# New engine lists and a listed buffer order for a packed attention-and-gating kernel

## The chip, the core and the metric

One core of one Trainium2 chip. The metric is the device time of one execution in microseconds (us), as the median of several runs. A profile of one further execution gives the rows that are read below. Five engines work at once: TensorE (PE, the matmuls; PEld are its weight loads), VectorE (DVE), ScalarE (ACT), GpSimd (POOL) and SyncE (SP, which issues nearly all DMAs). Each runs its own list of instructions strictly in the order written; between engines there are only semaphores.

## What is computed

```python
def phi(x):                       # q and k: (4, 4, 1088, 32), r = 8
    a = einsum('rd,bhsd->bhsr', S1, x); b = einsum('rd,bhsd->bhsr', S2, x)
    return einsum('bhsi,bhsj->bhsij', a, b).reshape(..., 64)
q_p, k_p = phi(q), phi(k)
kv = einsum('bhsf,bhsd->bhfd', k_p, v);  z = sum(k_p, axis=2)
x  = (q_p @ kv) / (q_p @ z + 1e-6)            # heads joined: (4, 1088, 128)
h  = maximum(x @ w_in, 0)                     # 1024 wide: u, v of 512 each
v_n = (v - mean(v)) / sqrt(var(v) + 1e-6)
v_s = einsum('ts,bsd->btd', w_spatial, v_n) + b_spatial
out = (u * v_s) @ w_out                       # (4, 1088, 128)
```

The spatial product (1088 x 1088 against 1088 x 512, for each of four batches) is most of the arithmetic.

## The kernel before

**Precision and pieces.** Every float32 operand of a large matmul is split into a high and a low part, and a product is three matmuls: high by high, low by high, high by low. ACT makes the high part by a cast, DVE or POOL the low part by a subtraction. The rows t of the spatial product come in three pieces c: 424, 332 and 332 columns wide; the 512 features in four blocks d; the summed index s in nine tiles kt of 128.

**One block.** For batch b, block d and piece c, `hidden` makes u on PE into the one PSUM bank of the kind `pu`, and ACT moves it to SBUF with a ReLU (`u210:1` is that move for b=2, d=1, c=0). `spatial` adds up nine steps in one of the two banks of the kind `sp` (`sp210:1` to `sp210:9`; a step is three matmuls, the last one two). `gate` multiplies the bank with u on DVE (`u210:2`, line 1173), which frees the bank, and splits the product (`gh210`, `gl210`); `out_mm` multiplies it with w_out (`po20:2` and the like). As there are two `sp` banks, the first step of a block waits for the gate of the block before last.

**Other names.** `pv` are the three matmuls of 512 columns for v, `vt32:1` the ReLU that takes them out of PSUM, `st` and `mv` their statistics, `vt32:4` to `:6` the normalisation, `vh`/`vl` its high and low parts. The two 332-wide pieces of batches 2 and 3 are computed with seven instead of eight products of halves (a Strassen scheme, line 1386); `tw` are the sums of weights for it, `t2`, `t3`, `tx`, `tkp`, `wl` their parts, `s` the sums of v, and `p10` one of the products. `kab`, `qab`, `tq`, `nd`, `xt` and `kv0` are the steps of the attention of batch 0, `pab` of batch 1.

**What sets the order.** `SEQ` is a text of 1904 names with an engine behind each (`u310:2@DVE`). `schedule` splits it into one list for each engine, fixed for good. A loop then walks through the five lists, keeps estimated times, and gives tiles their buffers; its result is the order in which the instructions are written. Where it sees PE waiting in the first 50 us, it puts matmuls of nothing (line 607) in between. The buffers of a kind are given out in one order for that kind:

```python
ts[:] = sorted((t for t in ts if t.users), key=lambda t: RANK.get(t.name, (t.users[0].n, t.users[0].first.index(t))))
```

With `RANK` empty this is the order in which the program text first uses the tiles.

Of the kernel before, what the change touches and what calls it, by code (L numbers as in the profile page):

```python
# [66 lines left out]
kv0:3@PE wt00:1@SP qab01:1@PE wt80:1@SP wi_x1:5@DVE tq00:1@PE kd0:1@DVE qa01:1@ACT wi_x1:6@DVE tq01:1@PE qpT00:1@ACT qab02:1@PE qp01:1@DVE qpT01:1@ACT
wi_x1:7@POOL qa02:1@ACT nd00:1@PE wi_x0:1@ACT qp02:1@DVE v93:1@POOL wih:1@ACT wi_x0:2@DVE tq10:1@PE rec0:1@DVE wil:1@POOL tq11:1@PE rec0:2@DVE
x320:1@DVE qpT10:1@ACT tq20:1@PE qpT11:1@ACT wi_x0:3@DVE xt0:1@PE nd01:1@PE xh0:1@ACT wi_x0:4@DVE xl0:1@DVE tq21:1@PE rec1:1@DVE pv000:1@PE rec1:2@DVE
wi_x0:5@DVE x321:1@DVE qpT20:1@ACT wTh:9@ACT qpT21:1@ACT bh:1@ACT wTh:1@ACT wTl:10@SP pv001:1@PE wi_x0:6@DVE wTh:2@ACT wt30:1@SP xt1:1@PE vt00:1@ACT  # L70
bl:1@DVE wt60:1@SP wi_x0:7@DVE nd02:1@PE vt00:2@ACT wt01:1@SP st000:1@DVE wTl:1@POOL xh0:2@ACT wt11:1@SP wTh:3@ACT xl0:2@DVE wt21:1@SP pv002:1@PE
wih:2@ACT rec2:1@DVE wTl:3@POOL eps:2@DVE wt31:1@SP rec2:2@DVE mv00:1@DVE pv010:1@PE x322:1@DVE wt70:1@SP vt00:3@ACT st001:1@DVE wt41:1@SP xt2:1@PE
wil:2@POOL vt01:1@ACT pv011:1@PE st002:1@DVE xh0:3@ACT mv00:2@DVE pv012:1@PE xl0:3@DVE wTl:9@POOL vt01:2@ACT mv00:3@DVE st010:1@DVE pu000:1@PE
sd00:1@ACT wTh:10@ACT qt10:1@SP st011:1@DVE wTl:2@POOL pv020:1@PE vt01:3@ACT qt11:1@SP u000:1@ACT rs00:1@DVE qt12:1@SP st012:1@DVE pv021:1@PE
# [4 lines left out]
vl00:3@DVE sp030:2@PE vt01:6@DVE sd02:1@ACT sp010:2@PE vh00:4@ACT vt01:5@DVE sp010:3@PE abT11:1@ACT sp000:3@PE rs02:1@DVE vl00:4@DVE vh00:5@ACT
sp020:1@PE wo_x:1@ACT t102:1@DVE sp030:3@PE wTl:12@DVE sp030:4@PE wTh:5@ACT t102:2@DVE vl00:5@DVE wt71:1@SP sp000:4@PE wTh:8@ACT qd10:2@SP sp020:2@PE  # L80
rs02:2@DVE vh00:6@ACT nm02:1@DVE sp020:3@PE vt02:4@DVE sp020:4@PE wTh:6@ACT vt02:5@DVE sp010:4@PE vh00:7@ACT vl00:6@DVE sp020:5@PE wTh:15@ACT
sp010:5@PE wTl:8@DVE wTh:13@ACT sp010:6@PE wo_x:2@DVE vt02:6@ACT sp030:5@PE vl00:7@DVE sp020:6@PE vh00:8@ACT sp030:6@PE wTl:6@DVE wTh:7@ACT sp000:5@PE
v90:2@POOL wTl:17@DVE sp000:6@PE wTh:12@ACT sp030:7@PE vh00:9@ACT vl00:8@DVE sp000:7@PE wt81:1@SP wTh:17@ACT sp020:7@PE vh00:10@DVE qd10:1@SP
wTh:16@ACT sp010:7@PE v92:2@ACT wTl:14@DVE sp030:8@PE wTl:15@DVE sp000:8@PE wt02:1@SP sp000:9@PE wTl:7@DVE sp020:8@PE wt12:1@SP wTl:19@DVE sp010:8@PE
sp000:10@PE wTl:5@DVE wt22:1@SP sp020:9@PE wTh:18@ACT sp000:11@PE wTl:18@DVE sp030:9@PE wTh:14@ACT sp020:10@PE sp010:9@PE wo_x:3@DVE v93:2@ACT
wt32:1@SP sp010:10@PE wTh:11@ACT wTl:16@DVE sp000:12@PE sp010:11@PE qd11:2@SP sp000:13@PE wTl:13@DVE wTh:19@ACT sp010:12@PE sp000:14@PE wo_x:4@DVE
qd11:1@SP abT12:1@ACT sp030:10@PE v91:2@ACT sp000:15@PE sp030:11@PE sp010:13@PE wt42:1@SP wo_x:5@DVE sp000:16@PE sp030:12@PE wt52:1@SP wo_x:6@DVE
sp010:14@PE sp020:11@PE sp030:13@PE wTl:20@DVE sp030:14@PE sp020:12@PE sp030:15@PE wo_x:7@POOL wt62:1@SP sp000:17@PE sp020:13@PE sp020:14@PE kt10:1@SP
sp010:15@PE sp000:18@PE kt11:1@SP sp030:16@PE sp010:16@PE u000:2@DVE wTl:21@POOL sp010:17@PE kt12:1@SP sp020:15@PE sp020:16@PE g000:1@ACT sp010:18@PE
sp020:17@PE woh:1@ACT sp030:17@PE u010:2@DVE sp001:1@PE wol:1@DVE sp001:2@PE g010:1@ACT sp001:3@PE wTh:20@ACT g000:2@DVE v10:1@SP sp001:4@PE  # L90
g010:2@DVE wt72:1@SP sp001:5@PE wTh:25@ACT wTl:22@DVE sp030:18@PE u030:1@ACT sp020:18@PE wTl:27@DVE sp001:6@PE wt82:1@SP wTh:22@ACT u020:2@DVE
po00:1@PE fa100:1@SP u030:2@DVE po00:2@PE v11:1@SP g020:1@ACT wTl:24@DVE pu001:1@PE g030:1@ACT g020:2@DVE fb100:1@SP kab10:1@PE g030:2@DVE fb100:2@SP
v12:1@SP po00:3@PE ka10:1@ACT u001:1@ACT po00:4@PE wTh:21@ACT wTh:23@ACT pu011:1@PE ob00:1@ACT kp10:1@DVE wTl:25@DVE sp011:1@PE ka11:1@ACT out:1@SP
wTh:26@ACT sp011:2@PE ka12:1@ACT fa101:1@SP wTl:28@DVE wTh:24@ACT sp001:7@PE u011:1@ACT kp11:1@DVE fa100:2@POOL sp001:8@PE fb101:2@SP wTh:27@ACT
sp011:3@PE fb101:1@SP wTl:29@DVE sp011:4@PE fh100:1@ACT sp011:5@PE fa110:1@SP fl100:1@POOL sp011:6@PE fb110:1@SP kp12:1@DVE sp011:7@PE fb110:2@SP
sp011:8@PE sp011:9@PE qd12:1@SP sp001:9@PE u011:2@DVE kv1:1@PE fa111:1@SP u001:2@DVE fa101:2@POOL fb111:1@SP pu021:1@PE kd1:3@DVE kd1:4@DVE kd1:1@DVE
sp021:1@PE qd12:2@SP kd1:2@DVE u021:1@ACT sp021:2@PE kvh1:1@ACT fb111:2@SP gh001:1@ACT sp031:1@PE kvl1:1@DVE fh101:1@ACT sp031:2@PE gl001:1@DVE
gh011:1@ACT sp031:3@PE fl101:1@POOL sp031:4@PE sp031:5@PE wTl:26@POOL nd100:1@PE fa120:1@SP nd101:1@PE fa110:2@POOL x3210:1@ACT fb120:2@SP po01:1@PE
x3210:2@ACT pu031:1@PE xn10:1@ACT fa121:1@SP x3210:3@DVE sp031:6@PE fh110:1@ACT kt20:1@SP sp031:7@PE xn10:2@ACT fl110:1@POOL fb120:1@SP sp021:3@PE
sp031:8@PE fa111:2@POOL fb121:2@SP sp021:4@PE sp021:5@PE kt21:1@SP x3210:4@DVE sp021:6@PE fb121:1@SP gl011:1@DVE sp021:7@PE xh1:1@ACT sp021:8@PE  # L100
fh111:1@ACT xl1:1@DVE sp031:9@PE u031:1@ACT fl111:1@POOL sp021:9@PE po01:2@PE u021:2@DVE pv100:1@PE fa120:2@POOL gh021:1@ACT pv101:1@PE gl021:1@DVE
vt10:1@ACT pu002:1@PE st100:1@DVE vt10:2@ACT pv102:1@PE st101:1@DVE nd110:1@PE vt10:3@ACT u031:2@DVE po01:3@PE mv10:1@DVE fh120:1@ACT nd111:1@PE
fl120:1@POOL sp002:1@PE x3211:2@ACT sp012:1@PE u002:1@ACT wTl:23@POOL sp012:2@PE x3211:1@ACT sp002:2@PE x3211:3@DVE fa121:2@POOL sp002:3@PE sp002:4@PE
fh121:1@ACT sp012:3@PE xn11:2@ACT fl121:1@POOL sp002:5@PE gh031:1@ACT sp002:6@PE xn11:1@ACT sp012:4@PE x3211:4@DVE sp002:7@PE xh1:2@ACT sp002:8@PE
xl1:2@DVE sp012:5@PE gl031:1@DVE sp012:6@PE sp002:9@PE sp012:7@PE u002:2@DVE pu012:1@PE st102:1@DVE pv110:1@PE mv10:2@DVE mv10:3@DVE pv111:1@PE
vt11:1@ACT gh002:1@ACT po01:4@PE st110:1@DVE vt11:2@ACT pv112:1@PE sd10:1@ACT st111:1@DVE ob01:1@ACT sp022:1@PE u012:1@ACT rs10:1@DVE sp022:2@PE
# [1500 lines left out]
```

## Time and profile before

| what | value |
|---|---|
| device time, median of 3 runs (lowest to highest) | 318.24 us (317.87 to 319.25) |
| the profiled execution | 320.65 us |
| its span, first to last instruction | 318.8 us |
| busy share of PE, DVE, ACT, POOL | 97%, 73%, 57%, 31% |
| mean granted clock of TensorE | 0.994 of full speed |

The profiled execution has 1.85 us outside its span, and took 2.4 us more than the median. A matmul's end is modelled in the profile, so that neighbours overlap; how far PE gets is read from the distance between two starts.

### The profile page before, as it was taken

The page shows a single profiled execution, that of the slowest core. Times are in us where ns is not written, and L with a number is a line of the kernel's source. Part 1 is how long each engine was busy: PE and PEld are TensorE (multiplying, and loading weights), DVE is VectorE, ACT ScalarE, POOL GpSimd, SP SyncE. Part 2 cuts the span into 40 slices and gives each one's busy share as a digit, 9 for nine tenths or more (in the row PEclk, how much of TensorE's full clock was granted, in tenths as well). Part 3 has the DMA queues.
Part 4 walks back from the last instruction along what each step waited for, and adds up shares of the span by engine and source line. Part 5 has one row for each costly group of instructions (what it writes and reads, how often), then busy time and mean ns, then how long its engine had stood idle before and what let it go on. Part 6 is the DMA issues. An engine that isn't in the chain of part 4 may idle for free.

```text
span 318.8 us, 6893 instructions
## 1 busy us (share of the span) xinstructions
PE 309.7 (97%) x2602; PEld 296.7 (93%) x2602; DVE 231.4 (73%) x525; ACT 182.7 (57%) x428; POOL 98.2 (31%) x130
## 2 busy tenths in 40 slices
...
GB/s 245 237 80 319 61 127 220 191 115 103 60 65 45 40 119 159 102 7 92 48 142 236 179 180 256 37 83 43 59 1 2 27 298 1 94 90 2 2 0 70
DMA packets 22989, 33.78 MB, mean 106 GB/s; under 512 B 3116, under 2 KB 21420, under 8 KB 22956
## 3 DMA queue, kind: packets, MB, share of 16 engines
...
q8 instruction: 20, 0.33, 0.4%
...
## 4 chain that ended last, share of the span: by engine, by line
PE 88%; DVE 5%; ACT 2%; DMA 2%; issue 1%; SPq 0%; ACTq 0%; DVEq 0%
PE sp L1136 14%; PE sp L1145 12%; PE sp L1138 12%; PE sd L1386 8%; PE sp L1386 7%; PE sd L575 3%; PE sd L577 3%; PE sd L576 3%; PE pu L575 2%; PE sp L1147 2%; PE po L575 2%; PE po L576 2%; PE po L577 2%; PE pu L577 2%; PE pu L576 2%; PE sd L787 2%
## 5 line engine op out<-in xcount | busy, mean ns | idle before, releaser
L1136 PE MATMUL sp<-wTh,vh 128*128 128x332 f32 (+1 forms) x286 | 94.2, 331 | 1.8 <-DVE u L1173 1.8
L1138 PE MATMUL sp<-wTh,vl 128*128 128x332 f32 (+1 forms) x240 | 79.1, 330 | 0.0
L1136 PEld LDWEIGHTS sp<-wTh,vh 128*128 128x128 f32 x286 | 54.3, 190 | 2.6 <-DVE u L1173 2.1
L1138 PEld LDWEIGHTS sp<-wTh,vl 128*128 128x128 f32 x240 | 45.4, 189 | 0.2
L1145 PE MATMUL sp<-wl,vh 128*128 128x332 f32 x128 | 39.6, 309 | 0.0
L1145 PE MATMUL sp<-wTl,vh 128*128 128x424 f32 x112 | 39.2, 354 | 0.0
L1173 DVE TENSOR_TENSOR u<-sp,u 128x332 f32<-128x332 f32 (+1 forms) x43 | 22.4, 523 | 18.8 <-PE sp L1147 12.8
L1129 ACT ACTIVATE u<-pu 128x332 f32<-128x332 f32 (+1 forms) x44 | 20.6, 469 | 17.4 <-PE pu L577 14.3
L978 DVE BATCH_NORM_STATS2 st<-vt 128x6 f32<-128x512 f32 x36 | 24.1, 685 | 9.0 <-ACT vt L976 8.9
L976 ACT ACTIVATE vt<-sd 128x512 f32<-128x512 f32 x36 | 21.3, 599 | 13.0 <-PE sd L577 12.6
L583 DVE TENSOR_TENSOR g<-u,g 128x332 fp32r<-128x332 f32 (+1 forms) x41 | 24.6, 599 | 5.1 <-ACT g L662 2.4
L953 DVE RECIPROCAL c<-c 128x384 f32<-128x384 f32 (+1 forms) x9 | 21.7, 2415 | 7.1 <-ACT c L951 7.0
L586 POOL TENSOR_TENSOR r<-pl,r 128x384 fp32r<-128x384 f32 (+1 forms) x18 | 17.5, 973 | 28.5 <-DVE g L583 11.3
L662 ACT CAST g<-u 128x332 fp32r<-128x332 f32 (+1 forms) x41 | 20.0, 488 | 10.6 <-DVE u L1173 8.0
L919 POOL TENSOR_TENSOR pl<-pl,pl 128x384 f32<-128x384 f32 (+1 forms) x18 | 17.4, 972 | 25.2 <-DMA pl<-qd 13.4
L1145 PEld LDWEIGHTS sp<-wl,vh 128*128 128x128 f32 x128 | 24.0, 188 | 0.0
L1050 ACT CAST vh<-vt 128x384 fp32r<-128x384 f32 x44 | 21.9, 511 | 1.6 <-DMA vt<-vd 1.5
L1052 POOL TENSOR_TENSOR vl<-vt,vh 128x384 fp32r<-128x384 f32 (+1 forms) x15 | 14.6, 979 | 23.7 <-ACT vh L1050 22.7
L1145 PEld LDWEIGHTS sp<-wTl,vh 128*128 128x128 f32 x112 | 21.3, 190 | 0.1
L1052 DVE TENSOR_TENSOR vl<-vt,vh 128x384 fp32r<-128x384 f32 (+1 forms) x29 | 17.2, 603 | 1.1 <-ACT vh L1050 1.1
L575 PE MATMUL pu<-xh,wih 128*128 128x332 f32 (+1 forms) x48 | 16.3, 339 | 1.1 <-ACT u L1129 0.9
L1394 DVE TENSOR_TENSOR sp<-sp,pl 128x332 f32<-128x332 f32 x24 | 12.2, 510 | 6.5 <-PE sp L1147 6.3
...
## 6 DMA issues: line engine op xcount, KB each, us to landing
...
```

The lines of the kernel that those rows point to most:

```text
L575: nc.tensor.matmul(o, ah, bh, start=start, stop=False)
L576: nc.tensor.matmul(o, ah, bl, start=False, stop=False)
L577: nc.tensor.matmul(o, al, bh, start=False, stop=stop)
L583: return lambda: nc.vector.tensor_tensor(out=o(), in0=a(), in1=bb(), op=ALU.subtract)
L978: op("DVE", 690, lambda stats=stats, t=t: nc.vector.bn_stats(out=stats.ap, in_=vt[:, t]), r=[(vt, t)], w=[stats])
L1050: op("ACT", c_act(384), lambda: nc.scalar.copy(out=vh[:, kk:kk + 3], in_=x()), r=vr, w=[(vh, g)])
L1052: return lambda: eng.tensor_tensor(out=vl[:, kk:kk + n], in0=x()[:, :n], in1=vh[:, kk:kk + n].bitcast(F32), op=ALU.subtract)
L1136: nc.tensor.matmul(sp[:, :cw], vh[:, kt], wTh[:, kt, cs], start=(kt == begin), stop=False)
L1138: nc.tensor.matmul(sp[:, :cw], vl[:, kt], wTh[:, kt, cs], start=False, stop=False)
L1145: nc.tensor.matmul(sp[:, :cw], vh[:, kt], w_lo(kt, c), start=False, stop=False)
L1173: op("DVE", c_dve(cw), lambda: nc.vector.tensor_tensor(out=u.ap, in0=sp[:, :cw], in1=u.ap, op=ALU.mult), r=[sp], w=[u])
L1386: nc.tensor.matmul(x[:, :cw], p, q, start=i == 0 and n == 0, stop=end and i == 3 and n == 2)
```

## The change

The same 1904 operations are issued. What differs is their order in all five lists, which engine does 118 of them (47 go from POOL to DVE, 43 from DVE to POOL, 12 from ACT to DVE, 8 from DVE to ACT, 4 from POOL to ACT, 4 from ACT to POOL), and `RANK`, which now lists the order in which the tiles of five kinds of buffers (kp, c, vl, g and r) are given out. The number of buffers, the tile shapes and the functions stay. The places that are spoken of below, from the new and the old text of `SEQ`, and a part of `RANK`:

```diff
--- before.py
+++ after.py
@@ -60,152 +60,172 @@
 AFTER_W = (7.0, 13.0, 13.0)
 
 SEQ = """
...
-kab02:1@PE ka02:1@ACT wi_raw0:1@SP wi_x1:4@DVE qab00:1@PE b32:1@SP kv0:1@PE kp02:1@DVE qa00:1@ACT wt20:1@SP eps:1@ACT kv0:2@PE wt10:1@SP qp00:1@DVE
...
-mv02:1@DVE nm00:1@DVE mv01:1@DVE wt61:1@SP mv01:2@DVE wTh:4@ACT vt00:4@DVE pu020:1@PE wt40:1@SP vt02:3@ACT st021:1@DVE wTl:4@POOL pab10:1@PE wt50:1@SP
-u020:1@ACT st022:1@DVE vh00:1@ACT pu030:1@PE vt00:5@DVE sd01:1@ACT abT10:1@ACT pab11:1@PE rs01:1@DVE vl00:1@DVE vh00:2@ACT pab12:1@PE vt00:6@ACT
...
-pu200:1@PE st310:1@DVE vt31:2@ACT pv312:1@PE tw5756:1@SP u200:1@ACT mv31:1@DVE vt30:5@DVE out:5@SP nd320:1@PE u200:2@DVE vt31:3@ACT xd1:1@SP
-pu210:1@PE vt30:4@DVE vt30:6@ACT nd321:1@PE tw1424:2@DVE x3232:1@ACT sp220:1@PE st311:1@DVE vh30:1@ACT sp220:2@PE st312:1@DVE x3232:2@ACT
-tw1756:2@POOL u210:1@ACT sp220:3@PE vh31:1@ACT tw5756:2@DVE sp210:3@PE wTh:29@ACT vh21:4@DVE sp220:4@PE mv31:3@DVE t2h0:1@ACT tw5424:2@POOL mv31:2@DVE
-x3232:3@DVE sd31:1@ACT sp210:4@PE xn32:1@ACT v91:4@POOL t3h0:1@ACT sp220:5@PE tw4424:2@POOL gh200:1@ACT sp210:5@PE xn32:2@ACT vh22:4@POOL sp220:6@PE
-rs31:1@DVE t131:1@DVE t131:2@DVE x3232:4@DVE sp210:6@PE rs31:2@DVE xh3:3@ACT sp220:7@PE nm31:1@DVE t3h1:1@ACT xl3:3@DVE sp220:8@PE vt31:6@ACT
-xh3:4@POOL sp210:7@PE xl3:4@POOL vt31:4@ACT sp210:8@PE t2h1:1@ACT sp210:9@PE vt31:5@ACT sp220:9@PE pv320:1@PE pu220:1@PE vt32:1@ACT pv321:1@PE
-txh:1@POOL pv322:1@PE vl30:1@POOL vl31:1@DVE wl1:1@DVE t2l0:1@DVE tw2424:1@SP txh:2@DVE out:6@SP tw2756:1@SP u210:2@DVE tw6424:1@SP gl200:1@DVE
-u220:1@ACT st320:1@DVE vt32:2@ACT tw6756:1@SP vh30:2@ACT pu300:1@PE st321:1@DVE vt32:3@ACT po20:1@PE tw2424:2@POOL u220:2@DVE gh210:1@ACT sp300:1@PE
-s100:1@DVE vh32:1@ACT sp300:2@PE u300:1@ACT mv32:1@DVE mv32:2@DVE vl30:2@DVE vh31:2@ACT sp310:1@PE st322:1@DVE tw2756:2@POOL sp310:2@PE mv32:3@DVE
-sp300:3@PE t2l1:1@POOL sd32:1@ACT wih:3@ACT rs32:1@DVE gl210:1@DVE sp310:3@PE gh220:1@ACT tw3424:1@SP pu310:1@PE t132:1@DVE tw6756:2@DVE p10:1@PE
-t132:2@DVE rs32:2@DVE p10:2@PE nm32:1@DVE vt32:4@ACT vt32:6@DVE p10:3@PE vt32:5@DVE p10:4@PE t2h2:1@ACT vl31:2@DVE sp300:4@PE vh31:3@ACT v90:5@POOL
-u310:1@ACT po20:2@PE vl31:3@DVE vh33:1@ACT wil:3@POOL sp310:4@PE vh31:4@DVE t3h2:1@ACT sp310:5@PE vh30:3@ACT txh:3@POOL txl:1@ACT sp300:5@PE
-vh32:3@ACT sp310:6@PE s300:1@POOL v91:5@ACT tw3756:1@SP vh33:3@ACT sp310:7@PE s100:2@POOL sp300:6@PE v92:5@POOL vh31:5@ACT sp310:8@PE tw6424:2@POOL
-wTh:30@ACT vh32:2@ACT vl32:2@POOL vl33:1@DVE gl220:1@DVE vl32:1@DVE vl30:3@DVE vl32:3@DVE tkp1:1@DVE vh30:4@DVE tw7424:1@SP po20:3@PE sp310:9@PE
-sp300:7@PE u310:2@DVE sp300:8@PE wl2:1@POOL vh32:4@DVE sp320:1@PE tw7756:1@SP sp320:2@PE t2l2:1@DVE tw3424:2@DVE sp300:9@PE wo_raw3:1@SP vl31:4@DVE
...
+ka01:1@ACT kp01:1@DVE kab02:1@PE kv0:1@PE ka02:1@ACT wi_raw0:1@SP qab00:1@PE kp02:1@DVE wt00:1@SP qa00:1@ACT wt80:1@SP eps:1@ACT qp00:1@DVE kv0:2@PE
...
+wTh:2@ACT mv01:1@DVE nm00:1@DVE pu010:1@PE vt00:4@DVE wt70:1@SP vt02:1@ACT vt00:6@DVE pv021:1@PE vh00:1@ACT vt00:5@DVE u010:1@ACT pv022:1@PE
+vl00:1@DVE vt02:2@ACT pu020:1@PE st011:1@DVE wTl:2@POOL vt02:3@ACT sp000:1@PE st012:1@DVE vh00:2@ACT sp010:1@PE wTl:12@POOL u020:1@ACT st020:1@DVE
+sp030:1@PE sp020:1@PE mv01:3@DVE mv01:2@DVE vl00:2@POOL pab10:1@PE st021:1@DVE sd01:1@ACT wTh:14@ACT pab11:1@PE rs01:1@DVE st022:1@DVE abT10:1@ACT
...
+sp200:9@PE sp210:5@PE tw5756:2@DVE u210:1@ACT u200:2@DVE nd320:1@PE vt30:6@ACT vt30:4@DVE nd321:1@PE x3232:1@ACT pu220:1@PE mv31:2@DVE wl1:1@DVE
+x3232:2@ACT tw5424:2@DVE sp220:1@PE t2h0:1@ACT tw2424:1@SP x3232:3@DVE gh200:1@ACT sp220:2@PE t2l0:1@POOL vh30:1@ACT sp210:6@PE t2h1:1@ACT tw2756:1@SP
+vh31:1@ACT sp210:7@PE t3h0:1@ACT sp220:3@PE t3h1:1@ACT st312:1@DVE sp210:8@PE xn32:2@ACT txh:2@POOL xn32:1@ACT mv31:3@DVE vl30:1@DVE sp220:4@PE
+sd31:1@ACT u220:1@ACT sp220:5@PE tw6424:1@SP x3232:4@DVE sp220:6@PE xh3:3@ACT sp210:9@PE xl3:3@DVE sp220:7@PE u210:2@DVE xl3:4@POOL sp220:8@PE
+xh3:4@POOL rs31:1@DVE gh210:1@ACT t131:1@DVE sp220:9@PE t131:2@DVE txl:2@ACT rs31:2@DVE sp300:1@PE nm31:1@DVE gl200:1@DVE pv320:1@PE vt31:5@DVE
+vl31:1@DVE pu300:1@PE vt32:1@ACT s300:1@DVE pv321:1@PE vt31:4@DVE u300:1@ACT vt31:6@ACT st320:1@DVE tkp1:2@POOL pv322:1@PE u220:2@DVE vt32:2@ACT
+pu310:1@PE t2l1:1@POOL tw6756:1@SP vh31:2@ACT st321:1@DVE sp300:2@PE vt32:3@ACT tw2424:2@POOL tw3424:1@SP sp310:1@PE st322:1@DVE p10:1@PE wTh:30@ACT
+mv32:2@DVE p10:2@PE s100:1@DVE mv32:1@DVE po20:1@PE mv32:3@DVE vl31:2@DVE sd32:1@ACT wih:3@ACT sp310:2@PE rs32:1@DVE vh32:1@ACT t132:1@DVE gl210:1@DVE
+sp300:3@PE txl:1@ACT tw2756:2@DVE u310:1@ACT sp310:3@PE tw6756:2@DVE vh30:2@ACT sp310:4@PE t132:2@DVE t2h2:1@ACT rs32:2@DVE wil:3@DVE sp310:5@PE
+nm32:1@DVE txh:1@DVE vt32:5@ACT pu320:1@PE vl30:2@DVE tw3756:1@SP gh220:1@ACT vt32:6@DVE p10:3@PE vh33:1@ACT vt32:4@DVE p10:4@PE tkp1:1@DVE sp300:4@PE
+vh32:3@ACT vl32:1@DVE vh31:3@ACT tw7424:1@SP po20:2@PE vl33:1@DVE v91:5@ACT sp310:6@PE vh30:3@ACT vl31:3@DVE v93:4@ACT sp300:5@PE vl30:3@DVE
+t3h2:1@ACT vh31:4@DVE vh33:2@ACT wl2:1@DVE sp300:6@PE vh32:2@ACT vh30:4@DVE tw7756:1@SP sp310:7@PE txh:3@DVE v90:5@ACT gl220:1@DVE sp300:7@PE
+wo_raw3:1@SP tw3424:2@DVE sp310:8@PE vl32:2@DVE sp310:9@PE vl32:3@DVE sp300:8@PE u310:2@DVE vh32:4@POOL sp300:9@PE vl33:2@DVE po20:3@PE t2l2:1@DVE
+sp320:1@PE u300:2@DVE sp320:2@PE tw6424:2@DVE gh300:1@ACT s100:2@DVE sp320:3@PE v92:5@ACT tw3756:2@DVE wTh:31@ACT sp320:4@PE vh31:5@ACT gl300:1@DVE
...
 """.split()
 
-RANK = {}
+RANK = {
+    "kp00": 0, "kp01": 1, "kp02": 2, "qp00": 3, "qp01": 4, "qp02": 5, "u000": 6, "u010": 7, "u020": 8, "u030": 9, "ob00": 11, "kp10": 10, "kp11": 12,
+    "kp12": 13, "kd1": 14, "kp20": 15, "kp21": 16, "kp22": 17, "kd2": 18, "kp30": 19, "kp31": 20, "kp32": 21, "kd3": 22, "tkp1": 23, "tkp0": 24,
...
+    "tkp2": 25, "qt00": 0, "qt01": 1, "qt02": 2, "qpT00": 3, "qpT01": 4, "x320": 6, "qpT10": 5, "qpT11": 7, "x321": 10, "qpT20": 8, "qpT21": 9,
+    "x322": 11, "qt10": 12, "qt11": 13, "qt12": 14, "x3210": 15, "xn10": 16, "x3211": 18, "xn11": 19, "x3212": 21, "xn12": 22, "qt20": 17, "qt21": 20,
...
+    "t2h3": 39, "gh231": 40, "gl231": 41, "gh232": 42, "gl232": 43,
+}
 
 END = B - 2
 LATE_GATES = {(END, 3, 1), (END, 3, 2)}
```

## Rows read from the trace of the kernel before

**Rows 1.** The page's first part: busy us, share and instructions of each engine.
```profile
PE 309.7 (97%) x2602; PEld 296.7 (93%) x2602; DVE 231.4 (73%) x525; ACT 182.7 (57%) x428; POOL 98.2 (31%) x130
```

**Rows 2.** Stretches: length; busy of PE, PEld, DVE, ACT, POOL (instructions); clock, DMA, GB/s.
```profile
9.02:31.62 22.60, 22.29 (x312) 18.05 (x311) 21.19 (x56) 18.89 (x43) 9.49 (x9) 1.00 0.65 207
31.62:206.22 174.60, 174.60 (x1533) 168.94 (x1532) 124.92 (x268) 108.93 (x252) 57.14 (x69) 1.00 0.38 117
196.28:211.04 14.76, 13.83 (x74) 13.02 (x73) 11.41 (x26) 11.56 (x25) 7.22 (x10) 1.00 0.38 123
211.04:225.32 14.28, 13.14 (x73) 12.79 (x71) 13.31 (x28) 8.77 (x22) 8.49 (x10) 1.00 0.09 25
218.15:224.61 6.46, 6.03 (x33) 5.69 (x31) 6.38 (x7) 3.60 (x10) 6.44 (x7) 1.00 0.09 26
226.43:229.84 3.41, 3.41 (x12) 3.19 (x11) 1.68 (x4) 1.62 (x4) 0.90 (x1) 0.50 0.33 94
```

**Rows 3.** Timeline of PE: start us, length us, instruction, idle time before and what ended it.
```profile
9.52 0.71 PE L607 MATMUL po<-u 128*128 128x128 f32 x4
...
29.41 0.55 PE L896 MATMUL sd<-c,sk 128*64 128x192 f32 x4
...
31.62 0.46 PE L1136 MATMUL po<-wTh,vh 128*128 128x424 f32 x1
...
193.07 0.31 PE L575 MATMUL po<-g,woh 128*128 128x332 f32 x1
...
208.63 0.40 PE L577 MATMUL sd<-wih,xl 128*128 128x512 f32 x1
209.96 0.46 PE L575 MATMUL pu<-xh,wih 128*128 128x424 f32 x1 [0.93 <-ACT u L1129]
...
211.21 0.35 PE L1136 MATMUL sp<-wTh,vh 128*128 128x424 f32 x1
...
214.57 0.35 PE L575 MATMUL pu<-xh,wih 128*128 128x424 f32 x1
...
223.84 0.35 PE L1145 MATMUL sp<-wTl,vh 128*128 128x424 f32 x1
225.97 0.46 PE L1136 MATMUL sp<-wTh,vh 128*128 128x424 f32 x1 [1.79 <-DVE u L1173]
```

**Rows 4.** The chain that ended last, in order of time: start us, us, what.
```profile
26.24 0.23 PE sd L577
...
241.22 1.78 PE sd L1386 x12
```

**Rows 5.** Timeline of DVE around the two waits of PE.
```profile
196.28 0.59 DVE L1173 TENSOR_TENSOR u<-sp,u 128x424 f32<-128x424 f32 x1
196.79 0.54 DVE L1014 TENSOR_SCALAR vt<-vt,mv,sm 128x512 f32<-128x512 f32 x1
197.25 0.50 DVE L1216 TENSOR_TENSOR pl<-pl,pl 128x332 f32<-128x332 f32 x1
197.66 1.28 DVE L978 BATCH_NORM_STATS2 st<-vt 128x6 f32<-128x512 f32 x2
...
200.38 2.12 DVE L953 RECIPROCAL c<-c 128x320 f32<-128x320 f32 x1
...
204.33 0.55 DVE L1052 TENSOR_TENSOR vl<-vt,vh 128x384 fp32r<-128x384 f32 x1
204.80 0.54 DVE L1216 TENSOR_TENSOR wl<-pl,wTh 128x332 fp32r<-128x332 f32 x1
...
207.75 0.51 DVE L1216 TENSOR_TENSOR xh<-pl,kt 128x332 fp32r<-128x332 f32 x1 [1.96 <-ACT vt L976]
...
220.49 3.26 DVE L1052 TENSOR_TENSOR vl<-vt,vh 128x384 fp32r<-128x384 f32 x3
...
225.32 0.60 DVE L1173 TENSOR_TENSOR u<-sp,u 128x424 f32<-128x424 f32 x1
```

251 lines of the change are left out of this document (126 added, 125 removed), and 14 rows, old and new, of the table RANK.

## The prediction

> **What bounds the kernel now.** The page's first part comes first: PE is busy 97% of the span, DVE 73%, ACT 57%, POOL 31% [rows 1]. All lists hold the same matmuls before and after, so time can come only from where PE stands still, runs at the lower clock or does filler. The stretches tell where that is [rows 2]. From 31.62 to 206.22 PE is busy for all of 174.60 us: nothing can be gained there, only lost. In the timeline of PE [rows 3] two waits follow. At 208.63 a matmul of 512 columns starts and the next one 1.33 us later; at 223.84 one of 424 columns starts and the next 2.13 us later. A matmul's own step is the distance of two starts: from 211.21 to 214.57 there are 18 of 424 columns, 0.187 us each [rows 3]; one of 512 columns takes 0.23, one of 332 takes 1.78 / 12 = 0.148 [rows 4]. So the waits cost 1.1 and 1.94 us. After the second the granted clock is 0.50, the 1.2 GHz level, from 226.43 to 229.84 [rows 2]. Half of these 3.41 us, 1.7, is what the clock costs. After the first wait the stretch from 211.04 to 225.32 shows 1.00.
>
> Why PE waits is seen in the timeline of DVE [rows 5]. The second wait ends 0.65 us after the gate at 225.32 starts, which is `u310:2`; `sp320:1` needs its bank. Since the gate at 211.04 (`u220:2`, where a stretch of rows 2 begins) 14.28 us had passed. In the middle, from 218.15 to 224.61, POOL is busy for 6.44 of 6.46 us with seven instructions [rows 2], and DVE's three `vl` at 220.49 take 3.26 us, where one alone takes 0.47 (204.33 to 204.80) [rows 5]: DVE is stretched by POOL. The first wait ends with ACT's `u220:1`, which needed a buffer that `gl200:1` frees; on DVE that stood behind `txh:2` at 207.75, which had idled for 1.96 us [rows 5].
>
> **The change, part by part.** `RANK` adds no instruction; it allows other orders, and where the buffers come free is in the lists. The five lists decide.
>
> *First wait.* In the new list `pu220:1` stands ahead of `sp220:1`, so that nine steps of `sp220` (8 x 0.56 + 0.37 = 4.9 us) and more lie between it and `pu300:1`; `txh:2` has gone to POOL. The price of `u220:1` is hidden under them. I take the 1.1 us as gone. Bounds: 1.1 back, if `gl200:1` is late, or nothing.
>
> *Second wait.* I set DVE's work from `u200:2` to `u310:2` against PE's from the end of `sp200:9` to `sp320:1`. Steps on DVE, by distance of starts [rows 5]: a 424-wide operation 0.51 (196.28 to 196.79), a normalisation 0.46, a 332-wide subtraction 0.41, statistics 0.64 (1.28 / 2), a 384-wide `vl` 0.47, the reciprocal 2.1. Estimates from these: 0.35 for 256 wide, 0.3 for `vh..:4`, 0.1 for the tiny ones. From `u200:2` up to `u220:2` the new list has 23 operations: three 424-wide 1.53, three normalisations 1.38, seven tiny 0.7, four of 332 or 320 wide 1.64, the reciprocal 2.1, two statistics 1.28, two `vl` 0.94, one 256-wide 0.35: 9.9 us. From there up to `u310:2` there are 34: three 424-wide 1.53, two statistics 1.28, eight tiny 0.8, five `vl` 2.35, seven 332-wide 2.87, five 256-wide 1.75, two normalisations 0.92, two `vh..:4` 0.6: 12.1. With the gate and its way to PE, 0.65, that is 22.7 us.
>
> PE has, up to the end of `sp220:9`, 43 matmuls of 424 columns and 6 of the small `nd32` (0.147): 8.9 us; from there 70 of 424 (13.1), nine of 512 (2.1) and twelve of 332 (1.8): 17.0. Together 25.9, which leaves DVE 3.2 us for three things. Its late start: PE moved on from `sp200:9` at 193.07 [rows 3], and the gate began at 196.28 [rows 5], 3.2 us late; the least is about 0.2 (a hand-over between the engines, an estimate). Between the gates of `sp132` and `sp200` the new list has 21 operations, at DVE's mean of 231.4 / 525 = 0.44 us [rows 1] 9.2 us, against some 12 us of matmuls; I take 0.6. Its waits: the old list idled 14.76 - 11.41 = 3.35 us and 14.28 - 13.31 = 0.97 [rows 2]; without the 1.96 of `txh:2` that is 2.4, which I take; least nothing. POOL beside it: the old list has ten POOL instructions in the second of these stretches, the new one two (`t2l1:1`, `tw2424:2`), and five in the first. DVE's seven operations from 218.15 to 224.61 were worth some 2.7 us by the steps above and were busy 6.38 [rows 2]: 3.7 us lost to 6.44 us of POOL, 0.57 for each. At a mean of 0.72 us (7.22 / 10, rows 2) the two cost 0.8; all seven, with 5.0 us, 2.9; none, nothing. I take 1.1, as in the first stretch POOL's 7.22 us [rows 2] left the steps of rows 5 at their usual size. The sum is 0.6 + 2.4 + 1.1 = 4.1 against 3.2: PE waits 0.9 instead of 1.94. Gain 1.0; bounds 1.94 (no wait) and a loss (below).
>
> *The clock.* A wait of about 0.9 us is like the first one, after which the clock stayed at 2.4 GHz. So the 1.7 us go too. If the wait is like the second one, they stay.
>
> *The head.* Before 31.62 PE works with short gaps. `kv0:1` now stands before `qab00:1`, where four filler matmuls took 0.5 us [rows 3]; the first spatial steps stand ahead of `pab10:1`, and from 29.41 to 31.62 [rows 3] PE did some 1.6 us of work (`pab` 1.05, `pu030` 0.56) in 2.2: 0.6 to be had. Against it, `wil:1` comes to DVE, and DVE is busy 21.19 of 22.60 us there [rows 2]; a 512-wide subtraction is some 0.6 (an estimate from 0.47 at 384), and it lies ahead of the first `xl0`. Bounds: 1.1 gained, 0.6 lost; I take a gain of 0.2, a little under the middle.
>
> *Elsewhere* 80 other operations change engine under 174.60 us of unbroken PE. I take nothing; the cover is that DVE is busy 124.92 and ACT 108.93 of these [rows 2]. If the cover is gone in one place, it costs a wait like the first, 1.1. At the end the last steps keep their order: nothing.
>
> **A rule that speaks against it.** The rows show that POOL stretches DVE by about 0.57 us for each us, when the two lie beside each other [rows 2, 5]. The Trainium skill, page "SBUF — State Buffer", section "Who interferes with whom", says that a DVE instruction with two SBUF inputs and a GpSimd instruction that reads SBUF block each other wholly, whichever starts second. By that rule POOL's whole 5.0 us of the new stretch could fall on DVE: PE would wait 0.6 + 2.4 + 5.0 - 3.2 = 4.8 us instead of 1.94, the lower clock would stay, and with the first wait gone and 0.2 from the head the time would be 318.24 + 2.9 - 1.1 - 0.2 = 319.8. The trace agrees only in part: from 196.28 to 211.04 POOL is busy for 7.22 us [rows 2], and the steps beside it keep their size [rows 5].
>
> **Sum.** 1.1 + 1.0 + 1.7 + 0.2 = 4.0. The profiled execution would go from 320.65 to 316.7. The median of the runs is 2.4 below it, so part of these losses may be absent there; I take off the whole: 318.24 - 4.0 = **314.2 us**. Without the part of the clock it would be 315.9.
>
> **The rivals.**
> - *DVE is as late as before.* The new list moves work from POOL onto DVE, from 8.6 us (26 operations at the same steps) to 12.1 between the last two gates; what POOL no longer takes away, DVE now does itself. Then the wait at `sp320:1` and the lower clock stay, and only the first wait goes: 318.24 - 1.1 = 317.1, or 316.9 with the head. For it: the margin of 3.2 us is no more than the old waits alone, 2.4, with little else. Against it: the old list gave away 0.97 idle and 3.7 to POOL in that stretch.
> - *DVE is later than before (slower).* The place is the same, `sp320:1`. If all 5.0 us of POOL fall on DVE, with the old late start of 3.2 and the waits of 2.4, the sum is 10.6 against 3.2: PE waits 7.4. With 1.94 and 1.1 gone and the clock's 1.7 staying, 318.24 + 4.4 = 322.6. It decides from where late start, waits and POOL reach 3.2 + 1.94 + 1.1 + 1.6 = 7.8 us. Against it, POOL's 7.22 us from 196.28 to 211.04 cost DVE next to nothing [rows 2, 5]. The rule of the page "SBUF — State Buffer" of the Trainium skill would make it likelier.
> - *Everything goes.* No wait at `sp320:1`, and the head gives 1.0: 318.24 - 1.1 - 1.94 - 1.7 - 1.0 = 312.5.
> - *The lists don't do what they say*, since the estimates by which they were chosen miss the chip's times. The new list would then wait in places that were unbroken, 1.1 or 2.1 us each: three of the former undo the gain, 317.5.
>
> **Chances.** Forecast 0.45; everything goes 0.2; as late as before, or undone by new waits, 0.23; slower 0.12. A change of under 0.5% (1.6 us: 316.65 to 319.83) is about what this kernel's measurement can't tell from none. The first two are faster by more: 0.65; the third is the same for nearly all: 0.23; slower 0.12. The range leaves out 1 in 10 at each end: from 312.3 (a little under "everything goes") to 319.6. The forecast's own range is 313.0 to 316.0.
>
> **What would show it.** Right: no wait ahead of `pu300:1`; the wait ahead of `sp320:1` under 1 us; a granted clock of 1.00 from 190 to 240; DVE's operations near 0.5 us each between `u220:2` and `u310:2`; the first spatial step earlier than 31.62. Wrong: a PE wait of 1.8 us or more around the gates of 200 to 230 us, a stretch at 0.50, or waits between 32 and 206, where there were none.

## The result, and the profile after

The kernel after takes 315.16 us (median of six executions, 313.96 to 316.06), the kernel before in the same comparison 319.01 (six, 317.87 to 320.37): a ratio of 0.9875, interval 0.9842 to 0.9909. 314.2 had been forecast. The profiled execution of the kernel after took 313.96 and was the fastest of its six, that of before took 320.65, more than any of its six; so the traces differ by 6.7 us where the medians differ by 3.85.

Page of the kernel after, first part, and from the second part the busy tenths of PE and the granted clock in 40 slices:

```profile
PE 306.6 (98%) x2598; PEld 295.3 (95%) x2598; DVE 228.7 (73%) x533; ACT 179.0 (57%) x424; POOL 93.0 (30%) x126
...
PE   7999999999999999999999999999999999999995
...
PEclk9999999999999999999999999999999999999999
```

Against [rows 1] DVE is busy for 2.7 us less and POOL for 5.2. No slice of PE but the first and the last is below nine tenths, and no clock is low. What PE still waits for is in the view of its waits (us in total, times, longest); all three lie in the first 14 us:

```profile
PE sd L618 <- DVE u L612: 1.3, 1, 1.3
PE sd L770 <- DMA kt<-in_kT: 0.4, 1, 0.4
PE pu L807 <- issue: 0.3, 1, 0.3
```

Stretches of the kernel after, columns as in [rows 2]: all that follows the head up to the end of `sp220`, from `u200:2` to `u220:2`, and from there to `u310:2`:

```profile
32.06:205.69 173.63, 173.63 (x1526) 168.07 (x1525) 122.80 (x260) 105.17 (x245) 58.65 (x73) 1.00 0.40 122
197.67:208.94 11.27, 11.27 (x61) 10.82 (x60) 10.57 (x25) 8.82 (x21) 2.58 (x5) 1.00 0.16 45
208.94:221.78 12.84, 12.84 (x73) 12.81 (x72) 12.41 (x35) 9.38 (x24) 2.26 (x3) 1.00 0.26 76
```

The second and third answer to the two stretches of [rows 2] that took 14.76 and 14.28 us. DVE now idles 0.70 and 0.43 us in them (before: 3.35 and 0.97), and POOL is busy for 4.84 us in both together (before: 15.71).

Timeline of PE after, at the two places of [rows 3]: `pu300:1` at 206.94 and `sp320:1` at 222.67 start 0.23 and 0.18 us after the matmul ahead of them, their plain steps.

```profile
206.71 0.39 PE L597 MATMUL sd<-wih,xl 128*128 128x512 f32 x1
206.94 0.35 PE L595 MATMUL pu<-xh,wih 128*128 128x424 f32 x1
...
222.49 0.35 PE L597 MATMUL po<-g,wol 128*128 128x424 f32 x1
222.67 0.35 PE L1156 MATMUL sp<-wTh,vh 128*128 128x424 f32 x1
```

Timeline of DVE after, against [rows 5]: `gl200:1`, `u220:2`, four `vl` in a row and `u310:2`. The four take 1.77 us now, where three took 3.26.

```profile
206.11 0.59 DVE L603 TENSOR_TENSOR g<-u,g 128x424 fp32r<-128x424 f32 x1
...
208.94 0.58 DVE L1193 TENSOR_TENSOR u<-sp,u 128x424 f32<-128x424 f32 x1
...
216.66 1.77 DVE L1072 TENSOR_TENSOR vl<-vt,vh 128x384 fp32r<-128x384 f32 x4
...
221.78 0.60 DVE L1193 TENSOR_TENSOR u<-sp,u 128x424 f32<-128x424 f32 x1
```

Of the signs that the prediction named, those of the waits, the clock and DVE's lengths came. The first spatial step came earlier too, at 28.41, as `sp000:1` now stands ahead of `pab10:1`; but the 31.62 of before was itself late. With the same old head it starts at 30.78 to 31.12 in the seven other traces that have it, here h3's; and before waited longer for the DMA of `kt` (first view; 0.3 to 0.5 us in three of the seven, none in four):

```profile
PE sd L750 <- DMA kt<-in_kT: 1.1, 1, 1.1
```

```profile
30.86 0.46 PE L1136 MATMUL po<-wTh,vh 128*128 128x424 f32 x1
```

### The profile page after: what moved, and what is told of

Same layout as the page of the kernel before. It is cut to its first block, busy times and chain, and to the rows that moved or that the text cites. A ratio compares the mean times of both kernels' runs of the same rounds, so it can differ in the third digit from the quotient of the medians.

```text
span 312.2 us, 6880 instructions
## 1 busy us (share of the span) xinstructions
PE 306.6 (98%) x2598; PEld 295.3 (95%) x2598; DVE 228.7 (73%) x533; ACT 179.0 (57%) x424; POOL 93.0 (30%) x126
## 4 chain that ended last, share of the span: by engine, by line
PE 94%; DMA 2%; SPq 1%; DVE 0%; ACT 0%; issue 0%
PE sp L1156 15%; PE sp L1158 13%; PE sp L1165 13%; PE sd L1406 9%; PE sp L1406 7%; PE sd L595 4%; PE sd L597 4%; PE sd L596 4%; PE pu L595 3%; PE pu L597 3%; PE po L595 3%; PE pu L596 3%; PE po L596 2%; PE po L597 2%; PE sp L1167 2%; PE sd L807 2%
## 5 line engine op out<-in xcount | busy, mean ns | idle before, releaser
L1158 PE MATMUL sp<-wTh,vl 128*128 128x424 f32 (+1 forms) x240 | 78.8, 328 | 0.0
L1165 PE MATMUL sp<-wTl,vh 128*128 128x424 f32 x112 | 38.1, 349 | 0.0
L603 DVE TENSOR_TENSOR g<-u,g 128x332 fp32r<-128x332 f32 (+1 forms) x41 | 22.3, 543 | 8.3 <-PE po L597 3.8
L1072 POOL TENSOR_TENSOR vl<-vt,vh 128x384 fp32r<-128x384 f32 (+1 forms) x15 | 13.5, 904 | 14.4 <-ACT vh L1070 9.4
L1072 DVE TENSOR_TENSOR vl<-vt,vh 128x384 fp32r<-128x384 f32 (+1 forms) x29 | 16.1, 569 | 1.7 <-ACT vh L1070 1.7
L777 DVE TENSOR_TENSOR kp<-ka,sd 128x768 f32<-128x768 f32 x15 | 13.9, 951 | 4.5 <-ACT ka L775 4.3
```

Of the source, the lines that this page charges most:

```text
L603: return lambda: nc.vector.tensor_tensor(out=o(), in0=a(), in1=bb(), op=ALU.subtract)
L1072: return lambda: eng.tensor_tensor(out=vl[:, kk:kk + n], in0=x()[:, :n], in1=vh[:, kk:kk + n].bitcast(F32), op=ALU.subtract)
L1158: nc.tensor.matmul(sp[:, :cw], vl[:, kt], wTh[:, kt, cs], start=False, stop=False)
L1165: nc.tensor.matmul(sp[:, :cw], vh[:, kt], w_lo(kt, c), start=False, stop=False)
```

## The experiments

Theory: the change gains because DVE is in time for the two waits at 208 and 224 us, and all else in the lists is worth nothing in sum. Rivals: the head gives about 1 us; or DVE's work is what it is, so that a wait taken away in one place comes back in the next.

| kernel | median us | ratio to before (interval) | lost ahead of `pu300:1` | ahead of `sp320:1` |
|---|---|---|---|---|
| after | 315.16 | 0.9875 (0.9842 to 0.9909) | 0 | 0 |
| h1, new head | 320.24 | 1.0052 (1.0026 to 1.0078) | 1.09 | 1.93 |
| h2, new from `sp132:9` on | 315.83 | 0.9910 (0.9882 to 0.9937) | 0 | 0 |
| e2, six from POOL to DVE | 318.83 | 0.9998 (0.9978 to 1.0018) | 1.09 | 0.52 |
| e1, after with eight to POOL | 316.70 | 0.9924 (0.9894 to 0.9955) | 0 | 0 |
| e3, `txh:2` later | 317.27 | 0.9934 (0.9910 to 0.9957) | 0 | 1.91 |
| e7, e2 with `vl32:2` later | 317.09 | 0.9921 (0.9896 to 0.9946) | 1.09 | 0.41 |
| e8, e3 and e7 together | 316.28 | 0.9889 (0.9864 to 0.9913) | 0 | 0.32 |
| h4, h1 with less filler | 320.02 | 1.0031 (1.0010 to 1.0053) | 1.10 | 1.95 |
| a2, after again | 315.02 | 0.9886 (0.9864 to 0.9907) | 0 | 0 |
| h3, old head | 315.10 | 0.9886 (0.9861 to 0.9911) | 0 | 0 |
| b1, old start | 314.33 | 0.9858 (0.9834 to 0.9881) | 0 | 0.2 |
| e9, e8 and the new tail | 315.24 | 0.9890 (0.9870 to 0.9911) | 0 | 0.2 |

"Lost" is the distance between two starts less the plain step, as in the prediction; [rows 3] give 1.10 and 1.94 for the kernel before. The kernel before was timed again beside each of the four groups of rows (after; h1 to e1; e3 to h4; a2 to e9); its medians were 319.01, 318.73, 319.08 and 318.48.

**Which part of the lists? h1 and h2.** Each joins the two orders at one place; `RANK` lists the buffers in the order in which the joined list first uses them.

```diff
 # h1
-SEQ = old
+SEQ = new up to pu030:1, then the old order of what is left
 # h2
-SEQ = old
+SEQ = old up to sp132:9, then the new order of what is left
```

> The new lists up to pu030:1 (some 32 us), from there on the old order for all that is left; buffers of the five kinds given out in the order of this mixture. My theory (the gain has two sources: the head, about 1 us, and the stretch from 196 to 230 us): both waits of the kernel before, 1.1 us ahead of pu300:1 and 1.9 us ahead of sp320:1, and the lower clock after the second stay; time 1.0 us under the kernel before (0.5 to 1.5). Rival (the head is the gain, the rest follows from it): both waits go, time 3 to 4.8 us under.

> The old lists up to sp132:9 (some 184 us), from there on the new order. My theory: what counts is the order from 196 us on; no wait ahead of pu300:1, none or under 1 us ahead of sp320:1, clock 1.00; time 3 to 4.8 us under the kernel before, without the head's 1.0. Rival (DVE must already arrive early: in the old lists it is 4.5 us late at the gate of sp132, in the new ones less than 2): a wait of 1 to 3 us ahead of sp310:1 or sp320:1 and perhaps the lower clock; time 0 to 2 us under. Second rival (the head is the gain): no change.

The lists from 183 us on hold most of the gain: 2.9 us, with 0.8 us of waits between 185.5 and 187.3 that come from the join. The head alone does not gain: h1 is 1.5 us slower than before, which was a miss. In h1 the join brings ten fillers of its own, 1.28 us, in PE's timeline:

```profile
33.55 1.28 PE L607 MATMUL po<-u 128*128 128x128 f32 x10
```

**h4** takes these away.

```diff
-FILL, FILL_TO, FILL_SPARE = 224, 50.0, 400
+FILL, FILL_TO, FILL_SPARE = 224, 30.0, 400
```

> As h1 (the new lists up to `pu030:1`, the old order from there), but no filler matmuls after 30 us of the plan: h1 had ten of them, 1.2 us, between 33.5 and 34.6 us, which neither the kernel before nor the one after has. My theory: they are what made h1 slower than before; without them the new head is worth nothing or a little: 318.9 us (318.4 to 319.4). Rival one: the new head gains the 1.0 us that the two traces differ by at the first spatial steps: 317.7. Rival two: the new head is itself slower, and the time stays at 320.2.

A miss again: the fillers had stood where PE waits anyway. In their place the timeline shows a wait for DVE's `vl`, 1.09 us over the plain step:

```profile
34.67 0.37 PE L1136 MATMUL po<-wTh,vh 128*128 128x424 f32 x1
35.95 0.46 PE L1138 MATMUL po<-wTh,vl 128*128 128x424 f32 x1 [0.90 <-DVE vl L1081]
```

So h1 and h4 measure their join. The head had to be asked the other way round, with the new lists behind an old head.

**Is the head worth anything? h3, b1 and a2.**

```diff
 # h3
-SEQ = new
+SEQ = old up to sp020:9, then the new order of what is left
 # b1, on PE
-kab02:1@PE kv0:1@PE qab00:1@PE kv0:2@PE
+kab02:1@PE qab00:1@PE kv0:1@PE kv0:2@PE
```

> The old lists up to `sp020:9` (some 40 us), then the new lists; no more filler than before. My theory: the head is worth nothing in sum (some 0.5 us gained from 20 to 32 us, some 0.3 lost ahead of 14 us): 315.3 us, within 0.6 of the kernel after. Rival: the head gives the 1.0 us that the two traces differ by at 32 us: 316.2. Rival two: the new head costs 0.9, as h4 has it: 314.3.

> The kernel after with the old order up to `nd00:1` only: on TensorE that puts `kv0:1` back behind `qab00:1`, with filler matmuls ahead of it; 20 to 32 us stay new. My theory: TensorE reaches `nd00:1` 0.1 to 0.4 us sooner and keeps the 0.5 us from 20 to 32 us: 314.9 us, 0.3 less than the kernel after. Rival: the place of `kv0:1` gains the 0.5 us of the four fillers that it replaces, as I predicted: 315.7.

> The kernel after once more, unchanged, with its trace: the profiled execution shown so far was the fastest of six (313.96 against a median of 315.16). My theory: its lead of 1.2 us lies ahead of 14 us (TensorE from `kab02` to `nd00:1` took 4.99 us there, 4.89 to 5.03 in the kernels with the old head, but 5.19 to 5.41 in three other kernels with the new head), and no new wait of over 0.3 us shows between 32 and 312 us: 315.2 us (314.5 to 315.8). Rival: waits such as the one at `sp310:1` (0.46 us of margin in that execution) come back in other executions, and the trace shows one.

With the old head the kernel takes 315.10 us, with the new one 315.02 in the same comparison: the head is worth nothing. b1 is the fastest kernel of the study, 314.33, but its interval (0.9834 to 0.9881) overlaps that of a2 (0.9864 to 0.9907), so that its lead of 0.7 over the kernel after is not shown. Its order on the other engines is the old one up to there, too. The start of b1 in PE's timeline, four fillers ahead of `qab00:1` and no gap behind; then that of the kernel after, without them, but with a gap in `kv0:3`:

```profile
8.96 0.71 PE L607 MATMUL po<-u 128*128 128x128 f32 x4
9.60 0.57 PE L750 MATMUL sd<-sk,c 128*64 128x64 f32 x12
10.10 1.09 PE L787 MATMUL pu<-v,kp 128*32 128x33 f32 x86
```

```profile
8.90 0.63 PE L807 MATMUL pu<-v,kp 128*32 128x33 f32 x48
9.46 0.57 PE L770 MATMUL sd<-sk,c 128*64 128x64 f32 x12
9.96 0.51 PE L807 MATMUL pu<-v,kp 128*32 128x33 f32 x34
10.72 0.47 PE L807 MATMUL pu<-v,kp 128*32 128x33 f32 x27 [0.26 <-issue]
```

The fillers stood where PE had to wait: what the list saves there it pays two steps later. The a2 run is half a miss. Its span is 1.0 us longer than the first trace of the kernel after; 0.3 us of that is there at `nd00:1` (13.70 against 13.39), but 0.48 lies at 263 us, a wait of the kind that the rival named:

```profile
263.88 0.42 PE L1406 MATMUL sp<-xl,vh 128*128 128x332 f32 x1 [0.32 <-DVE u L1193]
```

**The first wait alone: e3.** The kernel before, one operation moved on DVE:

```diff
-t2l0:1@DVE txh:2@DVE u210:2@DVE gl200:1@DVE st320:1@DVE
+t2l0:1@DVE u210:2@DVE gl200:1@DVE txh:2@DVE st320:1@DVE
```

> The kernel before, with one operation moved: `txh:2` stands on VectorE's list behind `gl200:1` instead of ahead of `u210:2`. My theory: VectorE no longer stands 1.96 us in front of two gates, `gl200:1` frees its buffer in time, the wait of 1.1 us ahead of `pu300:1` goes, and the wait ahead of `sp320:1` stays at 1.7 to 2.1 us, because that one comes from the stretch after it: 317.6 us against 318.7 (317.2 to 318.1). Rival: the wait only moves (VectorE's other work sets the time of `gl200:1` or of `sp320:1`): the second wait grows to about 3 us and the time stays at 318.7 within 0.5.

Right. DVE's timeline in e3: the gate `u210:2` waits 0.22 us instead of standing behind an idle 1.96, `gl200:1` is done by 207.2, and `txh:2` follows it at 207.13. PE's timeline shows the second wait as large as before, 2.10 between starts:

```profile
205.22 0.60 DVE L1173 TENSOR_TENSOR u<-sp,u 128x424 f32<-128x424 f32 x1 [0.22 <-PE sp L1147]
205.74 1.47 DVE L583 TENSOR_TENSOR g<-u,g 128x424 fp32r<-128x424 f32 x1
207.13 0.49 DVE L1216 TENSOR_TENSOR xh<-pl,kt 128x332 fp32r<-128x332 f32 x1
```

```profile
221.82 0.35 PE L1145 MATMUL sp<-wTl,vh 128*128 128x424 f32 x1
223.92 0.46 PE L1136 MATMUL sp<-wTh,vh 128*128 128x424 f32 x1 [1.75 <-DVE u L1173]
```

The median falls by 1.8 us (interval 1.4 to 2.9), where the traces show 1.1: for the rest they show no cause.

**The second wait alone: e2, then e7.** In e2 six operations of the stretch before `u310:2` go from POOL to DVE, as in the new lists. In e7 one of them moves six places down DVE's list as well, and `RANK` lists the buffers in that order; place and `RANK` are not told apart.

```diff
 # e2
-wil:3@POOL txh:3@POOL s300:1@POOL s100:2@POOL tw6424:2@POOL vl32:2@POOL
+wil:3@DVE txh:3@DVE s300:1@DVE s100:2@DVE tw6424:2@DVE vl32:2@DVE
 # e7: e2, and on DVE
-vl32:2 vl33:1 gl220:1 vl32:1 vl30:3 vl32:3 tkp1:1 vh30:4 u310:2
+vl33:1 gl220:1 vl32:1 vl30:3 vl32:3 tkp1:1 vl32:2 vh30:4 u310:2
```

> The kernel before with one change: six subtractions between 218 and 225 us (wil:3, txh:3, s300:1, s100:2, tw6424:2, vl32:2) go from POOL to DVE, at the places where the plan has them. My theory (POOL beside DVE stretches DVE by more than the work it takes off): the six cost DVE 2.3 us, and some 4 us of stretching go; u310:2 comes 1.5 to 2 us earlier, the wait ahead of sp320:1 falls from 1.9 us to under 0.5, the clock stays at 1.00, the wait ahead of pu300:1 stays; time 2 to 3.6 us under the kernel before. Rival (DVE is short of time, more work makes it later): the wait grows to about 4 us, time 2 us over.

> The kernel before with the six operations moved from GpSimd to VectorE as in the run before, and `vl32:2` set behind `tkp1:1` in VectorE's list, so that VectorE does not stand 1.22 us for ScalarE's `vh32:2` ahead of `vl33:1` and `gl220:1` (the buffers are listed so that this order is possible). My theory: it was the order on VectorE that ate what the move gained; now no wait ahead of `po20:3` (1.36 us in that run) and at most 0.5 us ahead of `sp320:1`, the first wait of 1.1 stays: 317.1 us (316.6 to 317.6). Rival: VectorE does the same work as before and GpSimd's stretching is only replaced by it: 1.2 us or more ahead of `sp320:1`, 318.3 to 318.9.

e2 fell: no change. Its timelines of DVE and PE say why:

```profile
221.03 1.42 DVE L1051 TENSOR_TENSOR vl<-vt,vh 128x384 fp32r<-128x384 f32 x2 [1.22 <-ACT vh L1049]
222.37 0.59 DVE L582 TENSOR_TENSOR g<-u,g 128x424 fp32r<-128x424 f32 x1
...
224.87 0.60 DVE L1172 TENSOR_TENSOR u<-sp,u 128x424 f32<-128x424 f32 x1
```

```profile
221.31 0.35 PE L574 MATMUL po<-g,woh 128*128 128x424 f32 x1
223.01 0.46 PE L575 MATMUL po<-g,woh 128*128 128x424 f32 x1 [1.36 <-DVE g L582]
...
225.52 0.46 PE L1135 MATMUL sp<-wTh,vh 128*128 128x424 f32 x1 [0.36 <-DVE u L1172]
```

With POOL quiet the operations have their plain lengths again (three `vl` and `tkp1:1` follow at 0.3 to 0.5 us each, where three `vl` took 3.26 in [rows 5]). But `vl32:2` stands ahead of `vl33:1` and `gl220:1` and idles 1.22 us for a cast of ACT, and PE's `po20:3` waits for `gl220:1`: 1.51 + 0.52 us lost instead of 1.94. In e7, with `vl32:2` out of the way, the wait at `po20:3` is gone and `sp320:1` waits this much:

```profile
223.56 0.46 PE L1135 MATMUL sp<-wTh,vh 128*128 128x424 f32 x1 [0.25 <-DVE u L1172]
```

318.83 became 317.09. Which engine does the work is worth nothing here without the order. One operation's place, with its `RANK`, is worth 1.7 us by the medians, 2.5 by the two ratios and 1.6 by the traces (1.51 + 0.52 lost against 0.41).

**Both waits: e8, and e9 with the tail.** e8 is e3 and e7 together: seven operations of 1904, and `RANK`. e9 has the new order from `sp230:1` on as well, on DVE and ACT too; on PE:

```diff
-sp230:4 po21:4 sp230:5 sp230:6 sp230:7 sp230:8 sp230:9 po22:4 po20:4 po20:5
+sp230:4 sp230:5 sp230:6 sp230:7 sp230:8 sp230:9 po21:4 po22:4 po20:5 po20:4
```

> The last two edits together on the kernel before: `txh:2` behind `gl200:1`, the six operations on VectorE, `vl32:2` behind `tkp1:1`. My theory: both waits go but for at most 0.4 us, no stretch of lower clock: 316.1 us (315.5 to 316.7), which would be two thirds of what the whole change gave, from eight places in a list of 1904. Rival: VectorE's lateness moves on to the next gate, and the time is 317.3 or more.

> e8 (the kernel before with both waits taken away by eight places in the lists) with the new order from `sp230:1` on as well: on TensorE `po21:4` stands behind `sp230:9` and no longer between its steps, so that it covers the last gate. My theory: the wait of 0.4 us ahead of `po20:4` goes: 315.9 us against 316.3 for e8. Rival: the end is set by the output transfer and the last operations of VectorE, and nothing changes: 316.3.

e8 reaches a ratio of 0.9889, and the whole change 0.9875 and 0.9886: a measurement can't tell them apart. So the two waits are the cause of the gain but for what the intervals hide, some 0.8 us to either side. For e9 the trace shows what was expected. The last steps, first in e8, then in e9; the matmuls of line 1193 start 0.54 and 0.15 us after the one ahead of them:

```profile
309.60 0.31 PE L576 MATMUL po<-r,wol 128*128 128x332 f32 x1
310.14 0.98 PE L1193 MATMUL po<-u,abT 128*128 128x324 f32 x4 [0.24 <-DVE u L1188]
```

```profile
308.94 0.32 PE L576 MATMUL po<-r,wol 128*128 128x332 f32 x1
309.09 0.93 PE L1193 MATMUL po<-u,abT 128*128 128x100 f32 x4
```

The times leave it open: the medians fall by 1.0 us, but those of before by 0.6 between the two comparisons, and the ratios are the same.

**POOL put back: e1.** The kernel after, with eight operations given to POOL.

```diff
-wil:3@DVE txh:3@DVE txh:1@DVE s300:1@DVE vl32:2@DVE tw2756:2@DVE tw6756:2@DVE wl2:1@DVE
+wil:3@POOL txh:3@POOL txh:1@POOL s300:1@POOL vl32:2@POOL tw2756:2@POOL tw6756:2@POOL wl2:1@POOL
```

> The changed kernel with one change: eight subtractions between the gates u220:2 and u310:2 (wil:3, txh:1, txh:3, s300:1, vl32:2, tw2756:2, tw6756:2, wl2:1) go from DVE to POOL. My theory: DVE is rid of 3.1 us of its own work, but 7.3 us of POOL beside it stretch it by 0.57 each, 4.1 us; u310:2 comes 1 us later, the changed kernel's margin of 0.3 us is used up, PE waits 0.5 to 1.5 us ahead of sp320:1; time 0.5 to 1.5 us over the changed kernel, 2.5 to 3 if the clock falls too. Rival (DVE is short of time): DVE comes 3 us earlier, no wait, time as the changed kernel.

The size came as expected, 1.5 us, in another place: at `sp310:1`, which has 210.05 - (208.94 + 0.65) = 0.46 us to spare in the kernel after and lost 0.91 here, since `u220:2` came late. Another 0.47 is lost at 227.92, where a matmul of line 596 waits for a `gl`. DVE's and POOL's timelines:

```profile
206.40 0.80 DVE L1025 SCALAR_TENSOR_TENSOR sm<-sm,sm 128x3 f32<-128x3 f32 x2
207.24 0.83 DVE L1025 SCALAR_TENSOR_TENSOR sm<-mv,sm 128x3 f32<-128x3 f32 x1
...
208.50 1.13 DVE L1034 TENSOR_SCALAR vt<-vt,mv,sm 128x512 f32<-128x512 f32 x1
...
210.47 0.68 DVE L998 BATCH_NORM_STATS2 st<-vt 128x6 f32<-128x512 f32 x1
211.08 0.57 DVE L1193 TENSOR_TENSOR u<-sp,u 128x424 f32<-128x424 f32 x1
```

```profile
206.45 0.74 POOL L1236 TENSOR_TENSOR kvl<-vt 128x256 f32<-128x256 f32 x1 [0.39 <-DVE sm L1025]
207.15 0.90 POOL L1236 TENSOR_TENSOR kp<-pl,xl 128x332 fp32r<-128x332 f32 x1
208.01 1.33 POOL L1236 TENSOR_TENSOR c<-pl,r 128x332 fp32r<-128x332 f32 x1
210.63 2.85 POOL L1236 TENSOR_TENSOR pl<-pl,pl 128x332 f32<-128x332 f32 x3 [1.29 <-DVE vt L1034]
```

An operation on three columns (207.24), which takes 0.16 us alone, ends with POOL's, at 208.07 and 208.05. The normalisation at 208.50 takes 1.13, where it takes 0.54 in the kernel after. The gate at 211.08 lies beside POOL too, and keeps its length.

## Why the prediction was right, and where its sizes were off

*First wait, 1.1.* Right in place and cause: e3 takes it away by moving `txh:2` alone. The size, 1.10, is that of the traces; e3's median fell by 1.8. Whether the other half of the account, `pu220:1` ahead of `sp220:1`, would do it alone was not tested.

*Second wait, 1.0 of 1.94.* The place and the account were right; the whole wait went. The term that was mis-sized is "its waits", 2.4 us: DVE idles 0.70 + 0.43 = 1.1. The rest, now measured: PE moved on from `sp200:9` at 196.73, the gate began at 197.67, 0.94 late (0.6 forecast); DVE was busy for 10.57 + 12.41 = 23.0 us (22.05 of work and 1.1 for POOL forecast); with the 0.65 of the gate that makes 0.94 + 1.1 + 23.0 + 0.65 = 25.7 against PE's 25.94 (25.9 forecast). DVE is 0.2 us early, where 0.9 late had been forecast. The late start was less to the point than it looked: in e8 it stays (PE leaves `sp200:9` at 192.48, `u200:2` starts at 195.69, 3.2 late), and `sp320:1` loses only 0.32.

*Why POOL stretches, and when not.* The prediction took POOL's cost for a rate, 0.57 us for each us. The fourteen traces of the study show that it hangs on the pair. Of DVE's operations, alone and beside a POOL instruction (over 0.1 us in common; alone is under 0.02):

```
operation, inputs           alone: n, median us   beside: n, median us   over 1.25 x alone
gate u..:2, PSUM and u       367   0.50            286   0.50               0 %
statistics st, one input     230   0.69            272   0.69               0 %
gl, u and g                  512   0.50             82   1.07              74 %
vl..:3, vt and vh            116   0.42             17   0.96              82 %
vl..:2, vt and vh            129   0.55             28   0.83              79 %
```

In the kernel after, POOL's three in a row from 208.57 to 211.20 lie beside a gate and three statistics, and cost nothing; in the old list its seven from 218.15 lay beside `vl` and `gl`. The Trainium skill, page "SBUF — State Buffer", section "Who interferes with whom", says that a DVE instruction with two SBUF inputs contends with a GpSimd instruction that reads SBUF, that one with at most one SBUF input does not, outside the modes in which it uses two ports, and that the two shut each other out for the whole of an instruction. The table agrees with who is hit, and 207.24 in e1 with how. Two kinds outside the table show that the number of inputs is not all: the normalisation, with one wide input, was slowed in five of six cases (0.54 alone, 1.3 beside; no run shows in which mode it ran), and `wl`, with two, in none of 19, all beside short casts of POOL. The price that the prediction drew from this rule, all 5.0 us of POOL on DVE, did not come: the list puts POOL beside other operations.

*The clock, 1.7.* This term was wrong for the median. The trace showed it, but the trace of before was not a usual execution: of the 53 executions of it that were timed in the study, nine have a mean granted clock of 0.995 or less (319.62 to 321.18 us), the other 44 one of 0.997 or more (317.82 to 319.98). The nine are 1.7 us above the others in the mean, so the price was right for an execution that pays it; the median is one that does not. The prediction saw that the median lay 2.4 us below the profiled execution and took off the whole all the same. A wait of that length brings the lower clock only in some executions: the trace of h4 has 1.95 us and then 0.50, as that of before; those of h1 (1.93) and e3 (1.91) have the wait and stay at 1.00. In h1 PE does 20 matmuls in the 3.41 us after it, where before did 12 [rows 2]:

```profile
226.45:229.86 3.41, 3.41 (x20) 3.40 (x20) 2.53 (x7) 1.95 (x5) 0.91 (x1) 1.00 0.33 94
```

What decides between the two, no run shows.

*The head, 0.2.* Worth nothing (h3); the time at which before began its spatial steps, 31.62, was late by 0.5 to 0.8 against the other traces with that head. *The end, nothing.* This was a misreading of the lists, as the order of the last steps did change: `po21:4` now covers the last gate, and the 0.40 ahead of `po20:4` went, by the trace. *Elsewhere, nothing.* Right: from 32.06 to 205.69 PE is busy for all of 173.63 us, and no new wait is seen there for the 80 other changes of engine.

So 4.0 = 1.1 + 1.0 + 1.7 + 0.2 came to 3.85, of which the traces bear out 1.1 + 1.94 + 0.4 = 3.4; the clock's term, too large, stood in for the rest of the second wait and for the end. That the sum came so near the measured gain is luck; that the two waits would go is not. What is left, 0.4, is within the interval.
